# First unit's k and q loaded first and turned ahead of the gates, a and U by VectorE alone, in an mLSTM cell with a multiplicative FFN

## The chip, the cores and the metric

The kernel runs on one core of a Trainium2 chip. TensorE multiplies matrices, VectorE, ScalarE and GpSimd work on tiles in the on-chip memory, SyncE issues transfers. Each engine works through its own list of instructions in order. The metric is the time of one execution on the device, in microseconds; several runs are taken and their median is given.

## What is computed

An mLSTM cell over 4 batches, 8 heads, 768 steps and a head size of 40, whose output, reshaped to 3072 tokens of 320, goes through a multiplicative FFN of width 1024:

```python
for t in range(S):
    m_new = np.maximum(f_gate[:, :, t] + m, i_gate[:, :, t])
    f_stab = np.exp(f_gate[:, :, t] + m - m_new)
    i_stab = np.exp(i_gate[:, :, t] - m_new)
    m = m_new
    C = f_stab[:, :, None, None] * C + i_stab[:, :, None, None] * np.einsum('bhd,bhe->bhde', vt, kt)
    n = f_stab[:, :, None] * n + i_stab[:, :, None] * kt
    h_tilde = np.einsum('bhde,bhe->bhd', C, qt)
    denom = np.maximum(np.abs(np.einsum('bhd,bhd->bh', n, qt)[:, :, None]), 1.0)
    y[:, :, t] = 1.0 / (1.0 + np.exp(-o_gate[:, :, t])) * h_tilde / denom
...
a = x @ w1
b = x @ w2
h = a * b @ w3
return (h @ w_out).astype(np.float32)
```

The inputs of the cell are 32-bit numbers. The four weight matrices are held as 64-bit numbers, and the kernel makes 32-bit ones of them itself.

## The kernel before

**Units and steps.** The cell is worked in chunks. A unit is 128 time steps of one batch with all 8 heads; there are 24 units, and unit n belongs to batch n mod 4. Inside a unit two chunks of 64 steps are done at once in the two halves of the partitions. The main loop (L709) runs over steps s: step s loads unit s + 2, makes the scores and the new state of unit s, the output of unit s - 1, and from step 4 on FFN products for units that are done. Front work before the loop prepares the gates for all units and the weights of unit 0.

**The gates** (L513 to L528). The gates of all heads lie in 96 partitions of 256 columns: a third of the time steps for each of 32 pairs of batch and head. `F` is the running sum of the forget gates in a chunk, `U` a running maximum, `a` the input gates, and `M` the maximum carried from chunk to chunk (`before` is M spread over a chunk). L524 and L525 take M from U and from a, L526 makes the maximum of U and F, L527 takes F from a, and L528 makes U = F - U. L525 and L527 run on GpSimd, the rest on VectorE. What leaves this part is a (`a - before - F`) and U (`F - max(U - before, F)`).

**What is made of them.** `pg` turns a gate tile on TensorE (`gate_cols`, L531), and ScalarE copies it: `aT` from a, later `wT` from w and `gT` from g. `spread` (L265) brings U to all partitions as `ub`, with 32 matmuls for a unit. `weights` (L275) makes `pw`: eight exponentials on ScalarE (L280) from `ub` and `aT`, and two masks on GpSimd (L282). `dec` (L539) gives `pick` on GpSimd (L547) and `pd` on TensorE, from which `decay` is copied (L555). `weighted` (L301) makes `vw` on GpSimd (L304) from v and `wT`.

**Turning k and q.** `turn` (L285) turns k and q of a unit on TensorE (`pt`, four matmuls each, through L95), and ScalarE copies them out as kT and qT (L299).

**The products of a step** (`quarter_work`, L312). For unit s: the scores `cell<-qT,kT`, then the new state's `cell<-vw,kbuf`; the multiplication of the scores by `pw` is VectorE's L355.

**Loads.** SyncE issues the loads. `load(n)` (L125) calls for k, q and v of a unit: each 160 KB, in pieces of 160 bytes (one head of one time step). `fetch` (L203) calls for a weight piece: 512 KB in rows of 4 KB, as 64-bit numbers. `scale` (L178) is ScalarE's part in making 32-bit numbers of a piece, `to_f32` (L180) VectorE's four operations; `scale_next` and `convert` take the pieces in the order in which they were called for. A transfer is issued only after the eighth before it in the list of SyncE's and ScalarE's transfers has landed, since they share eight semaphores in turn; in the front all of these have landed by then.

**Order.** TensorE's instructions keep the order in which they are written (L84). From L511 to step 31 the other engines keep theirs as well (`keep_order`, L499). So the list of ScalarE in the front is, before the change: L178 on the first piece, `dec`, `aT` (two copies), L178 on the second piece, the exponential of w (L544), eight exponentials of `pw`, kT, qT, `wT`, decay, g, L178 on the third piece. TensorE's list: `pg` for aT, `ub`, `pd`, `pt` of k and q, `pg` for wT, the products of unit 0, `pg` for gT, `ub` of units 1 and 2, `pt` of unit 1. SyncE's list: forget gates, weight pieces 1 and 2, k, q, v, o of unit 0, weight pieces 3 to 5, k, q, v, o of unit 1, three stores of U, then the loads of unit 2.

Of the kernel before, what the change touches and what calls it, by code (L numbers as in the profile page):

```python
# [10 lines left out]
AF = mybir.ActivationFunctionType  # L11
OP = mybir.AluOpType
# [4 lines left out]
def kernel(  # L17
# [26 lines left out]
    nc = tc.nc  # L44

    B, H, S, D = q.shape
    L = 64
# [29 lines left out]
    def mps(shape, name):  # L77
        pool = banks.pop(0)
        banks.append(pool)
        return pool.tile(shape, FP, name=name, tag="m")  # L80
# [10 lines left out]
    def mm(out, lhsT, rhs, start=True, stop=True):  # L91
        in_order(nc.tensor.matmul(out, lhsT=lhsT, rhs=rhs, start=start, stop=stop))  # L92

    def transpose(out, in_, n=P):
        in_order(nc.tensor.transpose(out, in_, ident[0:n, 0:n]))  # L95
# [6 lines left out]
    NB, NBQ = 4, 3  # L102
    N_DVE = 10
    q_all = const.tile([P, NBQ * H * DP], FP, name="q_all")
    qbuf = [q_all[:, i * H * DP:(i + 1) * H * DP].rearrange("p (h d) -> p h d", d=DP) for i in range(NBQ)]
    kbuf = [const.tile([P, H, DP], FP, name=f"kbuf{i}") for i in range(NB)]
    vbuf = [const.tile([P, H, D1], FP, name=f"vbuf{i}") for i in range(NB)]
    ident = const.tile([P, P], FP, name="ident")
    state = [[const.tile([P, NP, D1], FP, name=f"state{b}_{i}") for i in range(3)] for b in range(B)]
    aT = const.tile([P, NT2, BH], FP, name="aT")  # L110
# [10 lines left out]
    def rows(src, n):  # L121
        c, b = divmod(n, B)
        return src[b, :, c * P:(c + 1) * P, :].rearrange("h p d -> p h d")

    def load(n):  # L125
        for dst, src in ((kbuf[n % NB][:, :, 0:D], k), (qbuf[n % NBQ][:, :, 0:D], q), (vbuf[n % NB][:, :, 0:D], v)):
            if src is not q or n < N_DVE:
                nc.sync.dma_start(out=dst, in_=rows(src, n))

# [10 lines left out]
    def load_o(n):  # L140
        o_t[n] = io.tile([P, H, D], FP, name="o_in", tag="o_in", bufs=4)
        nc.sync.dma_start(out=o_t[n], in_=rows(o_gate, n))  # L142
# [24 lines left out]
    def raw_tile(n, pieces):  # L167
        raw = idle.pop(0) if idle else wst.tile([128, n, 2], U32, name="raw", tag="raw", bufs=4)
        for r, src in pieces:
            dst = raw[r].rearrange("p n two -> p (n two)")  # L170
            if len(src.shape) == 3:
                dst = dst.rearrange("p (m n) -> p m n", m=2)
            nc.sync.dma_start(out=dst, in_=src)  # L173
        return raw

    def scale(raw):
        hi = raw[:, :, 1].bitcast(FP)
        nc.scalar.activation(out=hi, in_=hi, func=AF.Prelu, scale=2.0 ** -111, alpha=2.0 ** 32)  # L178
# [15 lines left out]
    def cols(c0, n):  # L194
        return slice(2 * c0, 2 * (c0 + n))
# [7 lines left out]
    def fetch(kind, i, part):  # L203

        if kind == "w12":
            c0 = part * CW
            if i < 2 * KF:
                wt, src = ((w1, w1_d), (w2, w2_d))[i // KF]
                ko = i % KF
                dst, pieces = wt[:, ko, c0:c0 + CW], [(every, src[ko * 128:(ko + 1) * 128, cols(c0, CW)])]  # L210
            else:
                dst, pieces = wr[:, c0:c0 + CW], [(slice(j * REM, (j + 1) * REM), src[KF * P:DM, cols(c0, CW)])
                                                  for j, src in enumerate((w1_d, w2_d))]
        elif kind == "wo":
            dst, pieces = wo[:, i, :], [(square, wo_d[j * CQ + i * 32:j * CQ + (i + 1) * 32, :])
                                        for j, square in enumerate(squares)]
        else:
            dst, pieces = None, [(square, w3_d[i * 128 + part * 64:i * 128 + (part + 1) * 64, cols(j * CQ, CQ)]
                                  .rearrange("(m r) n -> r m n", m=2)) for j, square in enumerate(squares)]
        pend.append((dst, raw_tile(dst.shape[-1] if dst is not None else CW, pieces), i, part))  # L220
# [5 lines left out]
    def scale_next():  # L226
        scaled.append(pend.pop(0))
        scale(scaled[-1][1])
# [56 lines left out]
    def turn(n):  # L285


        if n >= N_DVE:
            for src, dst, name in zip(turned_in[n % 2], (kT_t, qT_t), ("kT", "qT")):
                dst[n] = sb.tile([128, NP, P], FP, name=name, tag=name)  # L290
                done = nc.vector.transpose(out=dst[n].rearrange("i p (r f) -> i p f r", f=4),
                                           in_=src[:, 32:TB].rearrange("i (p f d) -> i p f d", p=NP, f=4)[:, :, :, 0:32])
            return done
        for src, dst, name in ((kbuf[n % NB], kT_t, "kT"), (qbuf[n % NBQ], qT_t, "qT")):
            pt = mps([128, NP, P], "pt")
            for p in range(NP):
                transpose(pt[:, p, :], src[:, 2 * p:2 * p + 2, :].rearrange("p a b -> p (a b)"))
            dst[n] = sb.tile([128, NP, P], FP, name=name, tag=name)
            nc.scalar.copy(out=dst[n], in_=pt)  # L299
# [149 lines left out]
    f_sb, a, F, U, on = (gates[0:RG, i * TC:(i + 1) * TC] for i in range(5))  # L449
# [4 lines left out]
    dec = const.tile([RG, GC], FP, name="dec")  # L454
# [7 lines left out]
        nc.scalar.dma_start(out=a[r], in_=i_gate.rearrange("b h s -> (b h) s")[:, cs])  # L462

    w3o_words = w3o.rearrange("p f d -> p (f d)").bitcast(U32).rearrange("p (n two) -> p n two", two=2)
    fetch("w12", 0, 0)
    fetch("w12", 1, 0)
    load(0)
    load_o(0)
    fetch("w12", 2, 0)
    idle += [w3o_words[:, i * CW:(i + 1) * CW] for i in range(2)]  # L470
    fetch("w12", 3, 0)
    fetch("w12", 4, 0)
    load(1)
    load_o(1)

# [33 lines left out]
    f3, F3, U3, a3, w3d = (x.rearrange("p (c t) -> p c t", t=L) for x in (f_sb, F, U, a, w))  # L509
    V = nc.vector  # L510
# [10 lines left out]
        if i + 1 < GR:  # L521
            V.tensor_copy(out=M[third[i + 1], 0:1], in_=M[r, GC:GC + 1])
    before = M[:, 0:GC].unsqueeze(2).to_broadcast([RG, GC, L])
    V.tensor_tensor(out=U3, in0=U3, in1=before, op=OP.subtract)  # L524
    nc.gpsimd.tensor_tensor(out=a3, in0=a3, in1=before, op=OP.subtract)  # L525
    V.tensor_tensor(out=U, in0=U, in1=F, op=OP.max)  # L526
    nc.gpsimd.tensor_tensor(out=a, in0=a, in1=F, op=OP.subtract)  # L527
    V.tensor_tensor(out=U, in0=F, in1=U, op=OP.subtract)  # L528
    for i, r in enumerate(third):
        nc.sync.dma_start(out=U_d[i * GC:(i + 1) * GC].rearrange("c r t -> r c t"), in_=U3[r])  # L530
    def gate_cols(src, dst, copy):  # L531
        pg = mps([P, GC // 2, GR, BH], "pg")
        for c in range(GC // 2):
            transpose(pg[:, c].rearrange("p g r -> p (g r)"), src[:, c * P:(c + 1) * P], RG)
        for c in range(GC // 2):
            copy(out=dst.rearrange("p (g c) r -> p c g r", g=GR)[:, c], in_=pg[:, c])

    scale_next()
    nc.scalar.activation(out=dec, in_=U3[:, :, L - 1], func=AF.Exp)  # L539
    gate_cols(a, aT, nc.scalar.copy)  # L540
    V.tensor_tensor(out=w3d, in0=a3, in1=U3[:, :, L - 1:L].to_broadcast([RG, GC, L]), op=OP.add)
    scale_next()
    convert()
# [2 lines left out]
    for i, r in enumerate(third):  # L546
        nc.gpsimd.tensor_tensor(out=pick[r, :, i, :], in0=pair[r].to_broadcast([BH, B * NP, GC]), op=OP.mult,  # L547
                        in1=dec[r].unsqueeze(1).to_broadcast([BH, B * NP, GC]))
    weights(0)
    pd = mps([P, B * NP * NT], "pd")  # L550
    for x in range(2):
        mm(pd[halves[x]], odd[:, x].to_broadcast([RG, L]), pick.rearrange("p j g c -> p (j g c)"))
    turn(0)
    gate_cols(w, wT, nc.scalar.copy)
    nc.scalar.copy(out=decay.rearrange("p j c -> p (j c)"), in_=pd)  # L555
    nc.scalar.activation(out=g, in_=U, func=AF.Exp)
# [152 lines left out]
    for s in range(len(n_up)):  # L709
        if B <= s + 3 < NU:  # L710
            load_u(s + 3)
        if s + 2 < NU:
            load(s + 2)
            load_o(s + 2)
# [118 lines left out]
```

## Time and profile before

| what | value |
|---|---|
| median of 5 runs | 449.81 us (448.23 to 450.38) |
| the five runs | 449.81, 450.23, 448.29, 448.23, 450.38 us |
| the profiled execution | 448.58 us |
| its span, first to last instruction | 446.9 us |
| TensorE busy | 428.5 us (96% of the span) |
| VectorE, ScalarE, GpSimd busy | 342.5, 134.9, 84.1 us |
| TensorE busy, 0 to 35 us / 35 to 61 us / 61 us to the end | 25.66 / 22.61 / 380.26 us |
| share of the 16 transfer engines busy, same stretches | 0.95 / 1.06 / 0.51 |

The span is divided into stretches in the last two rows: of the 18.4 us in which TensorE is idle, 9.3 lie in the first 35 us, 3.4 in the next 26, and the rest later. The transfer engines are all but full for the first 61 us. A share can pass 1, since packets of one engine overlap.

A line of the timeline has the start of a group of instructions, its duration, the engine, the line of the program, the operation, the tiles written and read, the shapes and a count. In brackets stands how long the engine was idle before, and what ended that. PEld is TensorE's loading of the stationary operand, SPq an issue on SyncE. A wait for several things is put down to the one that came last by the profile, and where that one had long been done, it was another. Where a helper issues all matmuls, they have its line (L92, L95) and are told apart by their tiles.

### The profile page before, as it was taken

What the parts mean: (1) busy time and instruction counts of PE and PEld (TensorE: products, weight loads), DVE (VectorE), ACT (ScalarE), POOL (GpSimd) and SP (SyncE); (2) the same over time, 40 slices, a digit from 0 to 9 for tenths busy, and PEclk for the clock granted to TensorE, in tenths of its full rate; (3) what the DMA queues carried; (4) which work ended last, traced back from release to release, by engine and by line L of the source; (5) the groups of instructions that cost most, each with busy time, mean ns of one, the idle gap of its engine ahead of it and who ended that gap; (6) DMA issues with size and microseconds to landing.
All of it is one profiled execution on the core that took longest, in us unless ns stands there. A gap on an engine that the chain in (4) does not pass through costs nothing.

```text
span 446.9 us, 12911 instructions
## 1 busy us (share of the span) xinstructions
PE 428.5 (96%) x5271; PEld 340.1 (76%) x5271; DVE 342.5 (77%) x703; ACT 134.9 (30%) x376; POOL 84.1 (19%) x156
## 2 busy tenths in 40 slices
PE   2998989998999999999999999999999999999997
PEld 2787778787778878787877878778778777777774
DVE  6698599999998988988876859668698776445800
ACT  3754364443542343143222321203211111001110
POOL 6352233333202220221122203202020000000000
PEclk9999999999999999999999999999999999999999
DMA  8998987989998886686663677374121120000001
GB/s 176 197 167 164 215 155 148 162 183 173 217 192 185 165 174 172 145 173 138 111 114 101 138 151 135 75 131 116 51 37 34 35 50 17 15 16 15 1 29 44
DMA packets 136554, 52.71 MB, mean 118 GB/s; under 512 B 109936, under 2 KB 127536, under 8 KB 136496
## 3 DMA queue, kind: packets, MB, share of 16 engines
q1 hardware_dynamic: 132896, 47.87, 54.7%
q10 hardware_dynamic: 3600, 4.03, 2.6%
q8 instruction: 41, 0.67, 0.7%
q14 instruction: 17, 0.14, 0.1%
HBM read 46.07 MB, written 5.80 MB: 116 GB/s over the span
## 4 chain that ended last, share of the span: by engine, by line
PE 87%; DMA 3%; SPq 3%; DVE 2%; ACT 1%; issue 1%; POOL 1%; DVEq 0%; ACTq 0%; POOLq 0%
PE cell L92 23%; PE pa L92 21%; PE po L92 14%; PE pb L92 14%; PE wp L92 7%; PE p L92 5%; DMA kbuf<-in_k_dram 2%; PE pt L95 2%; PE px L95 1%; DMA raw<-in_moe_w_dram 1%; SPq L173 1%; SPq L142 1%; DVE pw L355 0%; DVE h L382 0%; PE ub L92 0%
## 5 line engine op out<-in xcount | busy, mean ns | idle before, releaser
L92 PE MATMUL pa<-xT,w 128*128 128x256 f32 x240 | 62.3, 391 | 0.7 <-ACT xT L440 0.7
L92 PE MATMUL po<-w3o,ab 128*128 128x320 f32 x224 | 61.8, 433 | 0.0
L92 PEld LDWEIGHTS po<-w3o,ab 128*128 128x128 f32 x224 | 42.4, 190 | 17.3 <-issue 0.4
L309 POOL TENSOR_TENSOR state<-state,decay 128x164 f32<-128x164 f32 x40 | 19.7, 492 | 183.6 <-DVE den L390 170.0
L92 PEld LDWEIGHTS pa<-xT,w 128*128 128x128 f32 x240 | 45.6, 195 | 9.0 <-ACT xT L440 1.6
L92 PE MATMUL pb<-xT,w 128*128 128x256 f32 x192 | 45.7, 381 | 1.5 <-ACT kT L299 1.5
L282 POOL TENSOR_SCALAR_AFFINE_SELECT pw<-pw 64x512 f32<-64x512 f32 x48 | 35.0, 729 | 52.5 <-ACT pw L280 51.0
L92 PE MATMUL cell<-w3o,ab 128*128 128x320 f32 x160 | 44.0, 432 | 0.0
L92 PEld LDWEIGHTS pb<-xT,w 128*128 128x128 f32 x192 | 36.6, 191 | 7.2 <-ACT kT L299 2.3
L280 ACT ACTIVATE pw<-pw,aT 128x64 f32<-128x64 f32 x160 | 40.3, 336 | 2.9 <-ACT o_sb L688 2.4
L633 DVE SCALAR_TENSOR_TENSOR a_sb<-pa,wo 128x512 f32<-128x512 f32 x12 | 8.3, 691 | 42.0 <-PE pa L92 42.0
L92 PEld LDWEIGHTS cell<-w3o,ab 128*128 128x128 f32 x160 | 30.4, 190 | 12.0
L585 ACT ACTIVATE a_sb<-pa 128x512 f32<-128x512 f32 x24 | 14.3, 597 | 77.1 <-PE pb L92 77.1
L92 PE MATMUL pa<-xT,wr 64*64 64x256 f32 x384 | 36.8, 386 | 0.0
L92 PE MATMUL pb<-xT,wr 64*64 64x256 f32 x384 | 36.2, 379 | 0.0
L92 PE MATMUL wp<-wo,w3T 128*128 128x320 f32 x128 | 35.9, 433 | 0.1
L382 DVE TENSOR_TENSOR h<-cell,h 64x164 f32<-64x164 f32 x96 | 31.3, 326 | 1.8
L92 PEld LDWEIGHTS wp<-wo,w3T 128*128 128x128 f32 x128 | 23.7, 190 | 9.2 <-DVE ab L586 0.4
L92 PEld LDWEIGHTS pa<-xT,wr 64*64 64x64 f32 x384 | 19.0, 132 | 14.4 <-issue 8.4
L688 ACT COPY o_sb<-po 128x320 f32<-128x320 f32 x14 | 6.0, 425 | 67.4 <-PE po L92 67.4
L586 DVE TENSOR_TENSOR ab<-pb,a_sb 128x512 f32<-128x512 f32 x24 | 16.1, 686 | 11.3 <-ACT a_sb L585 11.3
L178 ACT ACTIVATE raw<-raw 128x512 f32<-128x512 f32 (+1 forms) x32 | 19.2, 625 | 12.8 <-DMA raw<-in_moe_w_dram 11.0
(124 smaller groups left out, 751.3 us busy)
## 6 DMA issues: line engine op xcount, KB each, us to landing
raw<-in_moe_w_dram SPq DMA_DIRECT2D x64, 128.0 KB, 3.5
pw<-U_d SPq DMA_DIRECT2D x40, 128.0 KB, 4.1
kbuf<-in_k_dram SPq DMA_DIRECT2D x24, 160.0 KB, 4.6
vbuf<-in_v_dram SPq DMA_DIRECT2D x24, 160.0 KB, 4.9
o_in<-in_o_gate_dram SPq DMA_DIRECT2D x24, 160.0 KB, 4.5
out_dram<-o_sb ACTq DMA_DIRECT2D x24, 160.0 KB, 1.8
raw<-in_moe_w_dram SPq DMA_DIRECT2D x7, 512.0 KB, 5.5
raw<-in_moe_w_out_dram SPq DMA_DIRECT2D x32, 80.0 KB, 2.9
```

What stands on the lines that cost most here:

```text
L92: in_order(nc.tensor.matmul(out, lhsT=lhsT, rhs=rhs, start=start, stop=stop))
L95: in_order(nc.tensor.transpose(out, in_, ident[0:n, 0:n]))
L142: nc.sync.dma_start(out=o_t[n], in_=rows(o_gate, n))
L178: nc.scalar.activation(out=hi, in_=hi, func=AF.Prelu, scale=2.0 ** -111, alpha=2.0 ** 32)
L280: nc.scalar.activation(out=pw[:, h, :], in_=src[:, h, :], func=AF.Exp, bias=aT[:, c, b * H + h:b * H + h + 1])
L282: nc.gpsimd.affine_select(out=pw[r], in_=pw[r], compare_op=OP.is_ge, fill=0.0, base=0, pattern=[[0, H], [1, L]], channel_multiplier=-1)
L309: nc.gpsimd.tensor_tensor(out=new, in0=old, op=OP.mult, in1=decay[:, b * NP:(b + 1) * NP, 2 * c + x:2 * c + x + 1] .to_broadcast([P, NP, D1]))
L382: nc.vector.tensor_tensor(out=part, in0=ph[x][halves[e]], in1=part, op=OP.add)
L585: nc.scalar.mul(out=a_sb, in_=pa, mul=UP ** -2)
L586: nc.vector.tensor_tensor(out=ab_t[gr][j][:, fs[0]:fs[-1] + 1, t0:t0 + a_sb.shape[-1]], in0=pb, in1=a_sb, op=OP.mult)
L633: nc.vector.scalar_tensor_tensor(out=out, in0=p, scalar=UP ** -2, in1=q, op0=OP.mult, op1=OP.add)
L688: nc.scalar.copy(out=o_sb, in_=po)
```

## The change

It has three parts, all in the work before the loop.

- SyncE's list begins, after the forget gates, with k and q of unit 0; then come weight piece 1, v, weight piece 2, o and the rest as before.
- `turn(0)` is moved ahead of `gate_cols(a, ...)`: on TensorE `pt` of k and q comes first of all, ahead of `pg` for aT; on ScalarE kT and qT come first. There `dec` now follows aT, and the scaling of weight pieces 1 and 2 follows `dec`, both ahead of the exponential of w.
- a and U are made by four operations on VectorE and none on GpSimd: `before` is added to F, F is taken from a, the lesser of F and U goes into `f_sb`, and U is subtracted from that.

```diff
-    def load(n):
-        for dst, src in ((kbuf[n % NB][:, :, 0:D], k), (qbuf[n % NBQ][:, :, 0:D], q), (vbuf[n % NB][:, :, 0:D], v)):
+    def load(n, which=slice(0, 3)):
+        for dst, src in ((kbuf[n % NB][:, :, 0:D], k), (qbuf[n % NBQ][:, :, 0:D], q), (vbuf[n % NB][:, :, 0:D], v))[which]:
...
+    load(0, slice(0, 2))
     fetch("w12", 0, 0)
+    load(0, slice(2, 3))
     fetch("w12", 1, 0)
-    load(0)
     load_o(0)
...
-    V.tensor_tensor(out=U3, in0=U3, in1=before, op=OP.subtract)
-    nc.gpsimd.tensor_tensor(out=a3, in0=a3, in1=before, op=OP.subtract)
-    V.tensor_tensor(out=U, in0=U, in1=F, op=OP.max)
-    nc.gpsimd.tensor_tensor(out=a, in0=a, in1=F, op=OP.subtract)
-    V.tensor_tensor(out=U, in0=F, in1=U, op=OP.subtract)
+    V.tensor_tensor(out=F3, in0=F3, in1=before, op=OP.add)
+    V.tensor_tensor(out=a, in0=a, in1=F, op=OP.subtract)
+    V.tensor_tensor(out=f_sb, in0=F, in1=U, op=OP.min)
+    V.tensor_tensor(out=U, in0=f_sb, in1=U, op=OP.subtract)
...
+    turn(0)
+    gate_cols(a, aT, nc.scalar.copy)
+    nc.scalar.activation(out=dec, in_=U3[:, :, L - 1], func=AF.Exp)
     scale_next()
-    nc.scalar.activation(out=dec, in_=U3[:, :, L - 1], func=AF.Exp)
-    gate_cols(a, aT, nc.scalar.copy)
     V.tensor_tensor(out=w3d, in0=a3, in1=U3[:, :, L - 1:L].to_broadcast([RG, GC, L]), op=OP.add)
     scale_next()
     convert()
...
-    turn(0)
     gate_cols(w, wT, nc.scalar.copy)
```

## The prediction

> **What bounds the kernel now.** I read the timeline of TensorE first, because TensorE is busy for 428.5 of the 446.9 us span and has work almost without a break from 8.17 us on. Columns here and below: start, duration (both us), engine, line, operation, tiles, count, and in brackets the idle time before it with what ended that.
>
> ```profile
> 8.17 0.58 PE L95 MATMUL pg<-ident,gates 96*128 96x96 f32 x2 [8.17 <-DMA kbuf<-in_k_dram]
> 8.68 1.98 PE L92 MATMUL ub<-gates,ident 96*64 96x64 f32 x32
> ...
> 15.33 1.09 PE L92 MATMUL cell<-vw,kbuf 64*64 64x41 f32 x32
> ...
> 20.72 1.11 PE L95 MATMUL pt<-ident,kbuf 128*128 128x128 f32 x4 [0.17 <-DMA kbuf<-in_k_dram]
> ```
>
> TensorE starts at 8.17 us. The bracket blames a load of k, but `pg` turns the gates and reads no k; the weight load of the same instruction is put down to GpSimd's L527, which ends at 8.12. The second unit's `pt` at 20.72 does wait for a load: its k was called for at 11.87 and took 8.8 us, so it lands at 20.67.
>
> ```profile
> 34.82 1.09 PE L95 MATMUL pt<-ident,kbuf 128*128 128x128 f32 x4 [0.40 <-DMA kbuf<-in_k_dram]
> ...
> 42.07 0.88 PE L92 MATMUL cell<-vw,kbuf 64*64 64x41 f32 x23 [1.53 <-issue]
> ...
> 46.05 3.78 PE L92 MATMUL pa<-xT,w 128*128 128x256 f32 x8 [0.57 <-ACT xT L440]
> ...
> 55.68 1.89 PE L92 MATMUL pa<-xT,w 128*128 128x256 f32 x8
> ```
>
> Two things matter here. At 34.82 TensorE waits 0.40 us for the fourth unit's k: the loads gate the front twice, and a delay of TensorE before that is swallowed up to these waits. And the same eight `pa` products take 3.78 us at 46.05 but 1.89 us at 55.68: until about 49.8 us TensorE works at half its later speed, although the row of granted clock shows 9s throughout.
>
> Next, ScalarE, which is a strict queue in this kernel:
>
> ```profile
> 9.05 0.68 ACT L178 ACTIVATE raw<-raw 128x512 f32<-128x512 f32 x1
> 9.63 0.41 ACT L544 ACTIVATE gates<-gates 96x256 f32<-96x256 f32 x1
> 10.77 1.74 ACT L280 ACTIVATE pw<-ub,aT 128x64 f32<-128x64 f32 x8 [0.73 <-PE ub L92]
> ```
>
> The first unit's exponentials (`pw`, L280) come behind the scaling of the second weight piece (L178). Today that piece is long there and `ub` is what they wait for. GpSimd follows them:
>
> ```profile
> 12.64 1.82 POOL L282 TENSOR_SCALAR_AFFINE_SELECT pw<-pw 64x512 f32<-64x512 f32 x2 [2.04 <-ACT pw L280]
> 14.54 0.73 POOL L304 TENSOR_TENSOR vw<-vbuf,wT 128x328 f32<-128x328 f32 x1
> ```
>
> The masks end at 14.46, `vw` at 15.27, and the products of `vw` start at 15.33. So the path in the front is `ub`, eight exponentials, two masks, `vw`, products.
>
> VectorE's gate chain, with GpSimd's L525 and L527 beside it:
>
> ```profile
> 6.82 0.72 DVE L526 TENSOR_TENSOR gates<-gates 96x256 f32<-96x256 f32 x1
> 7.57 0.83 DVE L528 TENSOR_TENSOR gates<-gates 96x256 f32<-96x256 f32 x1
> 8.50 0.42 DVE L541 TENSOR_TENSOR gates<-gates 96x256 f32<-96x256 f32 x1
> ```
>
> An operation of 96x256 takes 0.42 us alone (L541, L524) and 0.72 to 0.83 beside GpSimd's. Last, the issues (tiles, count, size, us from issue to landing):
>
> ```profile
> vbuf<-in_v_dram SPq DMA_DIRECT2D x1, 160.0 KB, 7.1
> ...
> kbuf<-in_k_dram SPq DMA_DIRECT2D x1, 160.0 KB, 4.7
> ```
>
> The first is the first unit's v, issued at 4.23: landed at 11.3. The second is the third unit's k, issued at 22.53 into an almost empty queue. The same view gives the landings of the others: first weight piece 2.18 + 4.4 = 6.6, second 2.65 + 5.5 = 8.15, k 3.12 + 6.2 = 9.3, q 3.60 + 6.9 = 10.5. They land in the order of issue, a weight piece some 1.5 us after its forerunner and a 160 KB load 0.8 to 1.2 us.
>
> **The change, part by part.**
>
> *a and U by VectorE.* Removed: GpSimd's L525 and L527. VectorE has four operations in place of three. It starts them at 6.36 as now. With nothing of GpSimd beside them each takes 0.42 us plus a gap of 0.04: a is ready at 6.36 + 0.46 + 0.42 = 7.24 (8.12 now), U at 8.16 (8.40 now). Gain: 0.88 us for a, 0.24 for U. Bound: were the 0.72 to 0.83 theirs even without GpSimd, a would come at 7.5 to 7.6 and U at about 9.2.
>
> *k and q called for first.* SyncE issues k at 2.18 and q at 2.65, then the first weight piece, v, the second piece, o. With the rows of the third unit (4.7 and 4.8 us) k lands at 6.9 and q at 7.45; the lower bound is the first piece's own 4.4 less the 0.3 to 0.7 by which a 160 KB step is shorter, some 6.0.
>
> *Turned ahead of the gates.* `pt` is 1.12 + 1.06 us on TensorE: 6.9 to 9.0 (or from 6.0 to 8.1). Then `pg` to 9.5 (8.6) and `ub`, 1.98 us, to 11.5 (10.6); now it ends at 10.66. So the gates' gain is eaten by `pt`, which stands ahead of them, and `ub` ends between the same time and 0.9 us later. The two ScalarE copies of kT and qT (0.59 + 0.58) fall into ScalarE's idle time before 8.4. On ScalarE `dec` now stands behind aT (0.38 us) and the turned copies: at some 10.1 in place of 8.43, so GpSimd's `pick` (1.88 us) ends at about 12.2 and `pd` (0.91) at 13.1, still ahead of the masks and of `vw`. The 2.2 us of `pt` taken out after 11.49 help nothing by themselves: `vw` decides there, as 14.46 for the masks against 14.37 for wT shows.
>
> *The second weight piece.* This is the term that decides. It moves from second to fifth in the queue. The same five transfers that end with v at 11.3 us now will end with this piece, so I take its landing R = 11.3. Bounds: 10.0, if the first two run as short as the shortest step above; 13.6, if both pieces cost the 2.65 us that later ones do (17.8 against 15.2, from 9.87 + 8.0 and 8.67 + 6.5). ScalarE's next entries are L178 on this piece, the exponential of w, then the eight exponentials: now 9.05 to 10.04, so 0.99 us after R. They start at 12.3 in place of 10.77: 1.53 us late. Behind them on ScalarE wait wT, decay and g; for them wait GpSimd's masks and `vw`, and for that TensorE. The masks may be shorter: 1.82 us beside VectorE's conversion, 1.45 at 20.70; I give back 0.2.
>
> *The sum.* The products of `vw` start 1.53 - 0.2 = 1.3 us late. TensorE reached 20.72 with 0.18 us to spare and 34.82 with 0.40; both are used up. That leaves 0.75 us at 34.82, and as TensorE is the path from there (the waits at 42.07 and 46.05 follow from its own work), 0.75 us at the end. The 42.07 wait of 1.53 us has no cause in the profile; were its end fixed in time, it would swallow all of it. VectorE's two conversions, 0.7 us later, still end before their next operation at 16.59, which is itself 1.3 us late. SyncE's later issues are held by the queue and not by compute, so the loads of the next units stay where they are.
>
> *Speed of TensorE.* TensorE is busy for all 5.61 us from 8.17 to 13.78 and 6.34 of 6.41 from 14.13 to 20.54, and stays at half speed; so I count no gain for a denser front. The Trainium skill ("TensorE: Matmul & The Clock Gate", Part 1: The HAM clock gate) says that one busy window of about 3.4 us brings the full rate. This trace disagrees: two longer stretches did not. By the rule, an earlier start at `pt` would raise the speed earlier, and the sum would be a gain where the row gives none.
>
> **Time.** The profiled execution took 448.58 us for a span of 446.9; the five runs have a median of 449.81 and lie between 448.23 and 450.38. All six average 449.25. I start half way between this and the median, at 449.5, and add 0.75: 450.3. A difference of 0.3% (1.35 us) is about what a measurement of this kernel can tell from no change.
>
> **The rivals.**
> - *The loads hide it* (0.13). If R is 10.7 or less, the delay is under 0.7 and the two waits for k swallow it: 449.5. For: those waits. Against: the queue's landing times. It can't gain, because k of units two and four land as before.
> - *The second piece comes later still* (0.34). The mechanism is the same wait on ScalarE, with R at 12.3 as its centre: 2.5 - 0.2 - 0.58 = 1.75 us, so 451.3, or 451.6 from the median. It decides as soon as R passes 11.9, 0.6 us beyond my value. For: later weight pieces take 2.65 us each, and v's issue now hangs 3.58 us in SyncE's queue with the second piece behind it. Against: early pieces took 1.5 us.
> - *TensorE is fast sooner* (0.15). Should the half-speed stretch end before the first `pa` group, that group falls from 3.78 to 1.89 us: 449.5 - 1.9 = 447.6. For: runs 2.15 us apart with nothing else in sight. Against: a front as busy as now did not do it.
>
> **How the numbers follow.** The forecast has 0.38; with the first rival, no change has 0.51. Slower by more than 0.3% 0.34, faster 0.15. The range goes from 448.4, where runs like the quickest shown meet a hidden delay, to 452.0, which takes in the second rival with a run as slow as the slowest.
>
> **What would show it.** Right: `pt` at 6 to 7 us, ScalarE idle before its second L178 until a weight piece lands at about 11.3, L280 at about 12.3, `vw` at about 15.9, `pt` of the second unit at about 22 with no wait for a load, and of the fourth at about 35.6. GpSimd's two operations gone and VectorE's four at 0.42 us. Wrong: L280 before 11; or `pt` of the fourth unit at 34.8; or `pa` products at 0.2 us each before 46.

## The result, and the profile after

The changed kernel takes 447.38 us (median of 31 runs, 445.47 to 449.86). The kernel before has 449.81 us (55 runs, 447.02 to 453.55). The ratio is 0.9949 with a 95% interval of 0.9936 to 0.9962: faster by 0.51%, some 2.3 us. The prediction said 450.3 us, and gave no change a chance of 0.51.

The profiled execution took 446.57 us, with a span of 444.9 us against 446.9.

```profile
PE 422.2 (95%) x5271; PEld 333.3 (75%) x5271; DVE 342.7 (77%) x704; ACT 133.9 (30%) x376; POOL 81.5 (18%) x154
```

The busy times hardly tell what happened. The timeline of TensorE does; its columns are those of the prediction's lines. Units are counted from 0 here: the prediction's second and fourth units are units 1 and 3.

```profile
5.55 1.09 PE L95 MATMUL pt<-ident,kbuf 128*128 128x128 f32 x4 [5.55 <-DMA kbuf<-in_k_dram]
...
8.21 1.98 PE L92 MATMUL ub<-gates,ident 96*64 96x64 f32 x32 [0.21 <-DVE gates L528]
...
15.82 1.09 PE L92 MATMUL cell<-vw,kbuf 64*64 64x41 f32 x32 [2.63 <-POOL vw L304]
...
20.97 1.12 PE L95 MATMUL pt<-ident,kbuf 128*128 128x128 f32 x4
...
33.46 0.66 PE L95 MATMUL pt<-ident,kbuf 128*128 128x128 f32 x4
...
39.05 0.56 PE L92 MATMUL cell<-vw,kbuf 64*64 64x41 f32 x23 [1.07 <-issue]
40.04 0.63 PE L95 MATMUL pt<-ident,kbuf 128*128 128x128 f32 x4 [0.43 <-DMA kbuf<-in_k_dram]
...
42.88 3.78 PE L92 MATMUL pa<-xT,w 128*128 128x256 f32 x8 [0.57 <-ACT xT L440]
```

Read it beside the lines of before. The products of `vw` start at 15.82 us in place of 15.33: the front is later, by 0.49 us. Unit 1's `pt` is still 0.25 us later (20.97 against 20.72). Then the sign turns: unit 3's `pt` starts at 33.46 against 34.82, unit 4's at 40.04 against 42.87, and the first `pa` group at 42.88 against 46.05, which is 3.17 us earlier. So the start of the kernel, which the change edits, got slower, and the gain shows only behind it, clearly from unit 3 on.

ScalarE shows the wait that the prediction was built on:

```profile
8.54 0.66 ACT L178 ACTIVATE raw<-raw 128x512 f32<-128x512 f32 x1
10.52 0.67 ACT L178 ACTIVATE raw<-raw 128x512 f32<-128x512 f32 x1 [1.32 <-DMA raw<-in_moe_w_dram]
11.09 0.41 ACT L545 ACTIVATE gates<-gates 96x256 f32<-96x256 f32 x1
11.39 1.70 ACT L280 ACTIVATE pw<-ub,aT 128x64 f32<-128x64 f32 x8
```

The second L178 stands idle 1.32 us for the second weight piece, and the exponentials (L280) start at 11.39 in place of 10.77: 0.62 us late. On VectorE, the four operations that make a and U take 0.42 us each. Two of them:

```profile
7.28 0.41 DVE L527 TENSOR_TENSOR gates<-gates 96x256 f32<-96x256 f32 x1
7.73 0.42 DVE L528 TENSOR_TENSOR gates<-gates 96x256 f32<-96x256 f32 x1
```

The view that explains the gain is SyncE's, which the prediction did not follow past 12 us. First before, then after; each duration is how long SyncE was held at that issue.

```profile
4.23 3.58 SPq L128 DMA_DIRECT2D vbuf<-in_v_dram  x1
7.85 0.78 SPq L142 DMA_DIRECT2D o_in<-in_o_gate_dram  x1
8.67 1.15 SPq L173 DMA_DIRECT2D raw<-in_moe_w_dram  x1
9.87 1.96 SPq L173 DMA_DIRECT2D w3o<-in_moe_w_dram  x3
11.87 0.86 SPq L128 DMA_DIRECT2D kbuf<-in_k_dram  x1
```

```profile
4.10 0.43 SPq L128 DMA_DIRECT2D vbuf<-in_v_dram  x1
4.58 0.67 SPq L173 DMA_DIRECT2D raw<-in_moe_w_dram  x1
5.30 0.43 SPq L142 DMA_DIRECT2D o_in<-in_o_gate_dram  x1
5.77 2.26 SPq L173 DMA_DIRECT2D raw<-in_moe_w_dram  x1
8.07 1.69 SPq L173 DMA_DIRECT2D w3o<-in_moe_w_dram  x3
9.81 0.63 SPq L128 DMA_DIRECT2D kbuf<-in_k_dram  x1
```

Before, the issue of v holds SyncE for 3.58 us, and unit 1's k is called for at 11.87. After, v's issue takes 0.43 us, the long hold, of 2.26 us, comes at the third weight piece, and unit 1's k is called for at 9.81: 2.06 us sooner. The rest of the list follows it. Unit 2's k is issued at 20.69 (22.53 before), unit 3's at 25.60 (28.72). By the trace's records of the landings, unit 3's k has landed in full at 31.75 us (34.69 before), unit 4's at 39.90 (42.56).

Not all of the 3.17 us reaches the end: from the first `pa` to the end of the span there are 402.0 us after and 400.9 before. About one microsecond of that is TensorE idle between 61 and 100 us (1.66 us after, 0.59 before), and the largest piece of it is a stop of 1.15 us before 87.28, of the kind that is explained below. It is not a constant of the change: the same stretch from the first `pa` to the end was 401.0 us when the changed kernel was profiled again (e14 below), and over the fourteen profiled executions it lies between 399.9 (e2) and 404.1 us (e9). So one profile shows what moved the first `pa`; what that is worth is read from the timed runs.

### The profile page after: what moved, and what is told of

Same layout as the page of the kernel before. It is cut to its first block, busy times and chain, and to the rows that moved or that the text cites. A ratio compares the mean times of both kernels' runs of the same rounds, so it can differ in the third digit from the quotient of the medians.

```text
span 444.9 us, 12907 instructions
## 1 busy us (share of the span) xinstructions
PE 422.2 (95%) x5271; PEld 333.3 (75%) x5271; DVE 342.7 (77%) x704; ACT 133.9 (30%) x376; POOL 81.5 (18%) x154
## 4 chain that ended last, share of the span: by engine, by line
PE 87%; DVE 3%; DMA 3%; POOL 2%; ACT 2%; issue 2%; SPq 1%; DVEq 0%; ACTq 0%; POOLq 0%
PE cell L92 23%; PE pa L92 22%; PE pb L92 14%; PE po L92 14%; PE wp L92 8%; PE p L92 5%; DMA raw<-in_moe_w_dram 1%; DMA q_all<-in_q_dram 1%; PE px L95 1%; PE pt L95 1%; POOL pw L282 1%; ACT pw L280 1%; DVE h L382 1%; DVE pw L355 1%; DVE ab L586 0%
## 5 line engine op out<-in xcount | busy, mean ns | idle before, releaser
L280 ACT ACTIVATE pw<-pw,aT 128x64 f32<-128x64 f32 x160 | 40.2, 337 | 2.9 <-ACT o_sb L688 2.4
L92 PE MATMUL cell<-vw,kbuf 64*64 64x41 f32 x704 | 16.4, 227 | 6.8 <-POOL vw L304 4.0
```

The costliest lines, as they stand in the source:

```text
L280: nc.scalar.activation(out=pw[:, h, :], in_=src[:, h, :], func=AF.Exp, bias=aT[:, c, b * H + h:b * H + h + 1])
```

## The experiments

In the expectations, Theory 1 is that the loads make the gain, Theory 2 that TensorE's speed does, Theory 3 that the wait for the second weight piece still costs time. 1a, 1b and 1c are three forms of Theory 1. Each kernel is set against runs of the kernel before on the same chip, whose median is given with it.

**One part at a time.** e1 is the new order of the loads alone:

```diff
+    load(0, slice(0, 2))
     fetch("w12", 0, 0)
+    load(0, slice(2, 3))
     fetch("w12", 1, 0)
-    load(0)
     load_o(0)
```

> The first part of the change alone: k and q of unit 0 called for ahead of the weight pieces, v between the two pieces; TensorE's and ScalarE's lists and the gates as before. Theory 1 (the loads: v's issue no longer hangs 3.58 us in SyncE's list, so SyncE calls for the later pieces and units some 2 us sooner, and the k of unit 3 lands near 31.8 us in place of 34.7): 2 us or more of the 2.4 us gain comes with this part alone, around 447.5 us against 449.7, even if TensorE stays at half speed until 46 us. Theory 2 (TensorE's speed: the gain comes from TensorE going to full speed near 24 us, which needs the turned list): no gain, 449 to 450 us, with cell products of 32 still at 1.1 us up to 46 us. Theory 3 (the wait for the second weight piece on ScalarE, as in the prediction, costs here as well): scaling of piece 2 starts near 10.5 us, and as ub ends at 10.66 nothing is lost by it.

446.66 us against 448.38, ratio 0.9961 (0.9937 to 0.9984). The whole change's ratio lies in this interval. Unit 1's k lands at 18.17, unit 4's at 40.17, the first `pa` at 43.48.

e2 is `turn(0)` ahead of the gates, with `dec` behind aT, and nothing else:

```diff
+    turn(0)
+    gate_cols(a, aT, nc.scalar.copy)
+    nc.scalar.activation(out=dec, in_=U3[:, :, L - 1], func=AF.Exp)
     scale_next()
-    nc.scalar.activation(out=dec, in_=U3[:, :, L - 1], func=AF.Exp)
-    gate_cols(a, aT, nc.scalar.copy)
...
-    turn(0)
     gate_cols(w, wT, nc.scalar.copy)
```

> The second part alone: turn(0) ahead of the gates on TensorE and ScalarE, dec and the two scalings moved behind, loads called for in the old order, gates shared with GpSimd. k and q land at 9.3 and 10.5 us as before, so pt of q ends near 11.5 and ub near 14. Theory 1: slower by 1 to 3 us (451 to 453 us), since the loads of later units stay where they are and the front is 3 us late. Theory 2: could be faster if the denser list after 9.3 us brings TensorE to full speed before 30 us; then 447 to 448 us.

448.44 us against 448.38, ratio 1.0002 (0.9983 to 1.0020). Theory 1's expectation of 451 to 453 us was a miss, and no gain came either. ScalarE now waits for unit 0's k to be turned, and the exponentials start at 13.87 us:

```profile
10.45 0.58 ACT L299 COPY kT<-pt 128x512 f32<-128x512 f32 x1 [6.95 <-PE pt L95]
...
13.87 1.74 ACT L280 ACTIVATE pw<-ub,aT 128x64 f32<-128x64 f32 x8
```

```profile
18.48 1.09 PE L92 MATMUL cell<-vw,kbuf 64*64 64x41 f32 x32 [2.24 <-POOL vw L304]
...
43.38 1.11 PE L95 MATMUL pt<-ident,kbuf 128*128 128x128 f32 x4
...
46.46 1.99 PE L92 MATMUL pa<-xT,w 128*128 128x256 f32 x8 [0.64 <-ACT xT L440]
```

The products of `vw` start at 18.48, 3.15 us later than before. Yet the first `pa` group starts at 46.46, only 0.41 us later, and the time does not change. The waits that TensorE had in before (0.17 us for unit 1's k, 0.40 for unit 3's, 1.53 at 42.07) are all gone in e2: they took up most of the delay. So a front that is three microseconds late cost nothing here.

e3 is a and U by VectorE alone:

```diff
-    V.tensor_tensor(out=U3, in0=U3, in1=before, op=OP.subtract)
-    nc.gpsimd.tensor_tensor(out=a3, in0=a3, in1=before, op=OP.subtract)
-    V.tensor_tensor(out=U, in0=U, in1=F, op=OP.max)
-    nc.gpsimd.tensor_tensor(out=a, in0=a, in1=F, op=OP.subtract)
-    V.tensor_tensor(out=U, in0=F, in1=U, op=OP.subtract)
+    V.tensor_tensor(out=F3, in0=F3, in1=before, op=OP.add)
+    V.tensor_tensor(out=a, in0=a, in1=F, op=OP.subtract)
+    V.tensor_tensor(out=f_sb, in0=F, in1=U, op=OP.min)
+    V.tensor_tensor(out=U, in0=f_sb, in1=U, op=OP.subtract)
```

> The third part alone: a and U by four operations on VectorE, none on GpSimd. All theories: a is ready near 7.3 us in place of 8.1 and U near 8.1 in place of 8.4, so pg starts at 7.3, ub ends near 10.2 and the first exponentials start 0.3 to 0.5 us sooner. Theory 1: swallowed by the waits for k of units 1 and 3 at 20.7 and 34.8 us, no change (449 to 450 us). Theory 2: no change unless TensorE's speed rises early.

449.68 us against 448.38, ratio 1.0027 (1.0007 to 1.0047): no gain, perhaps a small loss. In its profiled execution the forget gates landed some 1.1 us later than before and VectorE's first scan started at 4.76 us; no reason for that was found, and whether it belongs to the edit stays open.

e6 is the loads with the turn, so the change without the gates.

> The first two parts together, the gates shared with GpSimd as before. The gates' part is worth 0.4 us in ub, which now waits for U and not for pt. Theory 1 and theory 2 both: near the changed kernel, 447.5 us within 0.5; ub starts at 8.4 to 8.7 us, but the exponentials still wait for the second weight piece at 10.5 us, so even these 0.4 us are hidden.

446.59 us, ratio 0.9960 (0.9942 to 0.9978), the same as e1. So the loads' order alone carries the gain, and the two other parts add nothing that can be measured.

**What in the loads' order?** e7 keeps the two weight pieces apart, as the change does, but puts the first one at the head and v behind the second: piece 1, k and q, piece 2, v, o.

```diff
-    fetch("w12", 1, 0)
-    load(0)
+    load(0, slice(0, 2))
+    fetch("w12", 1, 0)
+    load(0, slice(2, 3))
     load_o(0)
```

> The kernel before with only one thing moved: the second weight piece goes between q and v (piece 1, k, q, piece 2, v, o), so no more than two loads of 160-byte pieces stand in a row, as in the change, but the first weight piece keeps the first place and k of unit 0 lands near 8 us. Theory 1a (long rows of 160-byte pieces move slowly, 23 ns a packet after the first thousand or so against 14 to 16; a 4 KB weight piece in between breaks the row): the whole gain of the loads part, o of unit 0 in near 11.1 us, the fifth weight piece near 17 and k of unit 1 near 18.2 (20.67 before), time 446.3 to 447.2 against 448.4 to 449.7. Theory 1b (what counts is that the small loads of k and q stand first): little or no gain, k of unit 1 near 20 us. Theory 2 (TensorE's speed): no gain of itself.

448.74 us against 448.94, ratio 1.0000 (0.9974 to 1.0025): no gain. SyncE is held for 3.13 us at the third piece and calls for unit 1's k at 11.62. Breaking up the row of small loads is not the cause; 1a falls.

e8 puts all four small loads ahead of both pieces.

```diff
+    load(0)
+    load_o(0)
     fetch("w12", 0, 0)
     fetch("w12", 1, 0)
-    load(0)
-    load_o(0)
```

> The kernel before with k, q, v, o of unit 0 called for ahead of both weight pieces: four loads of 160-byte pieces in a row, and all of them first. Theory 1a: no gain in the loads, k of unit 1 at 19.8 us or later and packets of 160 bytes at 20 ns and more from the second thousand on; and as both weight pieces land near 10 to 11.5 us, the exponentials of unit 0 start 0 to 1.5 us late; time like before or up to 0.3% slower. Theory 1b (small loads first): k of unit 1 near 18.2 us and a gain like that of the loads part alone, 0.4%.

447.76 us, ratio 0.9982 (0.9956 to 1.0009): not settled as a time. The loads did come early, against 1a and as 1b has it (unit 1's k is issued at 8.85, unit 4's lands at 39.17), but TensorE then stood still for 2.76 us in the middle of a group, and its first `pa` is at 45.67:

```profile
41.69 0.88 PE L92 MATMUL cell<-vw,kbuf 64*64 64x41 f32 x23 [2.76 <-issue]
```

The 1.53 us before 42.07 in the kernel before is a stop at the same product (the tenth of its group of 32), and after has one of 1.07 us there too. None has a releaser in the timeline, but the trace's records of the transfers show what they wait for: each ends 1.2 to 1.6 us after the end of a transfer of 16 KB which the trace calls "instruction" (it ends at 40.22 us in e8, at 40.45 in before, at 37.81 in after). The same holds for all 26 stops of 0.3 us or more that TensorE makes with no releaser behind the first 14 us of the fourteen profiled executions. They come at few places of its list, above all before the 10th or the 23rd to 24th product of a `cell<-vw,kbuf` group, and where the transfer came sooner, as in e2 and e9, there is no stop at these places. That is TensorE waiting for its own instructions, which come through the same transfer engines as the loads. What decides when that transfer runs was not found.

e11 and e12 part "k and q first" (1b) from "a weight piece late in the list" (1c). e11 has piece 1 first, then k, q and v, then piece 2, o. e12 has k and q first, then both pieces, v, o.

```diff
     fetch("w12", 0, 0)
-    fetch("w12", 1, 0)
     load(0)
+    fetch("w12", 1, 0)
     load_o(0)
```

> The kernel before with one thing moved: the second weight piece goes behind v (piece 1, k, q, v, piece 2, o). The first weight piece keeps the first place. Theory 1c (depth of the queue: SyncE hangs while too many 160-byte pieces are queued; what is still queued when it comes free for the third weight piece decides whether the transfer engines run short at 12 to 14 us; a weight piece late in the list keeps the queue deep): gain in the loads, k of unit 1 at 18.2 to 19.0 us, engines full from 10 to 14 us. Theory 1b (k and q first of all): no gain in the loads, k of unit 1 at 20.2 us or later, as in the run with the pieces apart. In both the second piece lands near 11.3 us and delays the exponentials of unit 0 by 0.5 to 1.5 us; time 448 to 449.5.

> The kernel before with the list k, q, piece 1, piece 2, v, o: k and q first of all, and the last two small loads behind both weight pieces. Theory 1c (depth of the queue): little gain, since v and o are all that is queued when SyncE comes free, as in the kernel before; k of unit 1 near 20 us, engines at 0.8 from 12 to 14 us. Theory 1b (k and q first): k of unit 1 near 18.2 us and a gain of 0.4%, as in the loads part.

e11: 446.89 us against 448.14, ratio 0.9972 (0.9953 to 0.9991). e12: 447.70, ratio 0.9992 (0.9977 to 1.0007). So e12, with k and q at the head, gains nothing that can be told from none and not the 0.4% of 1b, and e11, without them there, gains: 1b falls. (The two intervals overlap; the profiles part the two more clearly, with unit 4's k landed at 42.39 us in e12 and 40.40 in e11.) SyncE in e12:

```profile
4.52 0.43 SPq L128 DMA_DIRECT2D vbuf<-in_v_dram  x1
...
6.07 3.10 SPq L173 DMA_DIRECT2D raw<-in_moe_w_dram  x1
...
10.95 0.72 SPq L128 DMA_DIRECT2D kbuf<-in_k_dram  x1
...
18.92 3.63 SPq L531 DMA_DIRECT2D U_d<-gates  x3
22.59 0.43 SPq L128 DMA_DIRECT2D kbuf<-in_k_dram  x1
```

and in e11:

```profile
3.76 2.23 SPq L128 DMA_DIRECT2D vbuf<-in_v_dram  x1
...
7.32 0.84 SPq L173 DMA_DIRECT2D raw<-in_moe_w_dram  x1
...
9.94 1.03 SPq L128 DMA_DIRECT2D kbuf<-in_k_dram  x1
...
18.98 1.92 SPq L530 DMA_DIRECT2D U_d<-gates  x3
20.94 0.43 SPq L128 DMA_DIRECT2D kbuf<-in_k_dram  x1
```

In both, SyncE is held for some microseconds, though at different issues; that the queue is full then is how the holds are read here, the trace shows only the holds. What differs is what lies in the queue meanwhile. The views by stretch of before and after show the transfer engines then (the last two columns are their mean busy share and the GB/s moved):

```profile
8.00:10.00 2.00, 1.83 (x26) 1.61 (x28) 1.83 (x5) 1.42 (x5) 1.25 (x4) 1.00 1.26 138
10.00:12.00 2.00, 2.00 (x21) 1.27 (x18) 1.84 (x4) 1.27 (x8) 0.60 (x1) 1.00 1.23 223
12.00:14.00 2.00, 1.78 (x9) 1.48 (x7) 1.87 (x3) 1.60 (x6) 1.31 (x2) 1.00 0.80 197
```

```profile
8.00:10.00 2.00, 1.79 (x34) 1.80 (x36) 1.30 (x4) 1.20 (x5) 0.93 (x3) 1.00 1.12 320
10.00:12.00 2.00, 1.28 (x10) 0.49 (x6) 1.84 (x4) 1.48 (x6) 0.00 (x0) 1.00 1.00 308
12.00:14.00 2.00, 1.19 (x33) 0.95 (x32) 1.90 (x4) 2.00 (x11) 0.72 (x2) 1.00 1.00 309
```

Before, the queue at 8 to 12 us holds v and o, 160 KB loads in pieces of 160 bytes: the engines are full but move 138 and 223 GB/s. They land by 11.8; the third weight piece, whose issue is over at 9.82, lands at 15.17, and between 12 and 14 us the engines are busy only 0.80 of the time. After, a 512 KB weight piece lies between and behind them, the engines stay full at 308 to 320 GB/s, the third piece's issue is over at 8.03 and it lands at 12.56. The share between 12 and 14 us is 0.75 in e7 and 0.87 in e12 (no gain), 1.04 in e11 and 1.09 in e8. That fits 1c. Why the engines run at 0.8 with fewer items in the queue was only argued, not shown.

Not all of 1c came true. Unit 1's k landed at 19.41 us in e11, later than the 18.2 to 19.0 that 1c asked for, and at 19.51 in e12, hardly apart; the third weight piece landed at 14.14 in e11 and at 13.60 in e12. The two runs come to the stores of U together (18.98 and 18.92 us) and part there: the stores hold SyncE for 1.92 us in e11 and 3.63 in e12, and unit 2's k is issued 1.65 us apart. So the runs show which orders bring the loads early, and not by what chain. They fit one description: with one small load or none behind the second weight piece (after, e1, e11, e8) the loads come early, with two or more (before, e7, e12) they come late.

**Is it TensorE's speed?** After's TensorE is at full speed from 24 to 41 us (its groups of 32 products take 0.66 us there in place of 1.09), so its speed is a rival to the loads. e9 adds 15 products of the identity with itself to the kernel before, from 1.6 us on, whose results nothing reads.

```diff
+    for _ in range(15):
+        mm(cell[0][:, 0, 0:P], ident, ident)
     f3, F3, U3, a3, w3d = (
```

> The kernel before with 15 products of ident with itself, whose results nothing reads, on TensorE from 1.6 us to about 8 us, when it was idle: they are to bring TensorE to full speed ahead of the front, with the loads as before. Theory 2 and the third rival of the prediction (TensorE's speed makes the gain): faster by 1.9 us or more, 446.5 to 448. Theory 1 (the loads): cell products of 32 take 0.65 us in place of 1.1 in the front, but k of units 1 to 4 still lands at 20.7, 27.2, 34.7 and 42.6, so TensorE only waits more; a gain of 0 to 0.8 us.

449.64 us against 448.94, ratio 1.0012 (0.9989 to 1.0035).

```profile
8.55 1.15 PE L92 MATMUL ub<-gates,ident 96*64 96x64 f32 x32
...
14.47 0.68 PE L92 MATMUL cell<-vw,kbuf 64*64 64x41 f32 x32 [1.21 <-POOL vw L304]
...
20.69 1.11 PE L95 MATMUL pt<-ident,kbuf 128*128 128x128 f32 x4 [1.74 <-DMA kbuf<-in_k_dram]
...
42.46 1.09 PE L95 MATMUL pt<-ident,kbuf 128*128 128x128 f32 x4 [1.60 <-DMA kbuf<-in_k_dram]
...
45.81 3.78 PE L92 MATMUL pa<-xT,w 128*128 128x256 f32 x8 [0.57 <-ACT xT L440]
```

TensorE is fast until 15.6 us (`ub` 1.15 us, not 1.98) and the products of `vw` start 0.86 us sooner. It then waits 1.74 us for unit 1's k and 1.60 us for unit 4's, and the first `pa` comes at 45.81. What TensorE wins, the loads take. This run speeds only the first 15.6 us; for the later stretch there are others. By the clock records e7 and e12 run fast from about 24 to 34 us too (0.63 and 0.68 us for 32 products at 25 us), without a gain, and e13 below has the earliest `pa` of all with TensorE at half speed from 30.3 to 40.5 us (1.04 us for 32 products at 37.37). Theory 2 falls.

**Does the wait for the second piece still cost?** e10 is the whole change with that piece scaled behind unit 0's exponentials.

```diff
     scale_next()
     V.tensor_tensor(out=w3d, in0=a3, in1=U3[:, :, L - 1:L].to_broadcast([RG, GC, L]), op=OP.add)
-    scale_next()
     convert()
...
     weights(0)
+    scale_next()
```

> The changed kernel with the scaling of the second weight piece moved behind the eight exponentials of unit 0 on ScalarE. This tests the step that the prediction took for decisive. If that wait sets the end: the exponentials start near 10.3 us in place of 11.4, the products of vw near 14.8 in place of 15.8, and the time falls by 0.5 to 1 us below the changed kernel, to 446.4 to 446.9 by the runs of the changed kernel so far. Theory 1: the second unit's turning can start no sooner than 18.1 us and later steps wait for k and q of units 3 and 4 (32 and 40.7 us), so the 1 us is swallowed and the time is that of the changed kernel within 0.3 us.

446.28 us against 448.94, ratio 0.9939 (0.9918 to 0.9960). The wait is gone:

```profile
9.70 0.41 ACT L544 ACTIVATE gates<-gates 96x256 f32<-96x256 f32 x1
10.59 1.75 ACT L280 ACTIVATE pw<-ub,aT 128x64 f32<-128x64 f32 x8 [0.48 <-PE ub L92]
```

The products of `vw` start at 14.85, 0.97 us sooner than after's, the first `pa` 0.37 sooner (42.51). The interval overlaps that of the change, so neither a gain of 0.5 us nor none is shown.

e13 is e10 with the three stores of U issued behind the third weight piece, ahead of unit 1's loads, which before they followed; that lets the later loads be issued sooner. e14 is the changed kernel again, on the same chip.

```diff
-    idle += [w3o_words[:, i * CW:(i + 1) * CW] for i in range(2)]
-    fetch("w12", 3, 0)
-    fetch("w12", 4, 0)
-    load(1)
-    load_o(1)
...
         nc.sync.dma_start(out=U_d[i * GC:(i + 1) * GC].rearrange("c r t -> r c t"), in_=U3[r])
+    idle += [w3o_words[:, i * CW:(i + 1) * CW] for i in range(2)]
+    fetch("w12", 3, 0)
+    fetch("w12", 4, 0)
+    load(1)
+    load_o(1)
```

> The changed kernel with the late scaling of the run before, and the three stores of U called for right behind the third weight piece in place of behind the loads of unit 1. In the changed kernel SyncE spends 3.2 us on these stores at 17.5 us while the queue runs empty (0.33 of the engines busy from 20 to 22 us). Theory 1 (the loads set the front): the loads of units 2 to 4 land 1 to 2 us sooner, k of unit 4 at 38 to 39 us in place of 39.9, and the time falls by another 0.5 to 1.5 us, to 444.5 to 446 us. If the loads no longer set the front after the change: the same as the changed kernel with late scaling, 446.3.

> The changed kernel itself once more, to be compared with the run beside it on the same chip: 446.4 to 447.4 us, 0.4 to 0.6% below the kernel before.

e13: 445.59 us against 448.14, ratio 0.9951 (0.9934 to 0.9968). e14: 446.58, ratio 0.9962 (0.9947 to 0.9977). e13's loads are the earliest of all and its first `pa` is at 41.48, but the two intervals overlap: whether it beats the change is not settled.

**All of them in one table.** The columns are read from each profiled execution: when SyncE issues unit 1's k, when unit 4's k has landed, when the first `pa` group starts; the ratio to the kernel before is from the timed runs.

| kernel | k of unit 1 issued | k of unit 4 landed | first `pa` | `pa` less landing | ratio |
|---|---|---|---|---|---|
| before | 11.87 | 42.56 | 46.05 | 3.49 | |
| e3 | 11.95 | 43.53 | 46.82 | 3.29 | 1.0027 |
| e2 | 11.79 | 42.28 | 46.46 | 4.18 | 1.0002 |
| e9 | 11.78 | 42.33 | 45.81 | 3.48 | 1.0012 |
| e7 | 11.62 | 42.98 | 46.42 | 3.44 | 1.0000 |
| e12 | 10.95 | 42.39 | 45.87 | 3.48 | 0.9992 |
| e10 | 10.29 | 39.23 | 42.51 | 3.28 | 0.9939 |
| e11 | 9.94 | 40.40 | 43.74 | 3.34 | 0.9972 |
| after | 9.81 | 39.90 | 42.88 | 2.98 | 0.9949 |
| e1 | 9.78 | 40.17 | 43.48 | 3.31 | 0.9961 |
| e6 | 9.68 | 39.66 | 43.18 | 3.52 | 0.9960 |
| e14 (the change again) | 9.47 | 40.00 | 43.37 | 3.37 | 0.9962 |
| e8 | 8.85 | 39.17 | 45.67 | 6.50 | 0.9982 |
| e13 (stores of U ahead of it) | 11.46 | 38.28 | 41.48 | 3.20 | 0.9951 |

In twelve of the fourteen the first `pa` follows the landing of unit 4's k by 3.0 to 3.5 us, whatever the front did. In eleven of these unit 4's `pt` starts 0.13 to 0.16 us after that landing, so it is the load that lets it go. The twelfth is before:

```profile
42.87 1.11 PE L95 MATMUL pt<-ident,kbuf 128*128 128x128 f32 x4
```

There `pt` follows the landing by 0.31 us and waits for nothing: the stop that ends at 42.07, with the 23 products behind it, ends last by some 0.2 us. Without that stop, as in e9, the load holds `pt` to about the same time. The two others are e2, whose front was three microseconds late, and e8, where the stop of 2.76 us ended last. Every kernel that issues unit 1's k by 10.3 us has unit 4's k by 40.4, and so has e13, which issues the three stores of U ahead of that k and not behind unit 1's loads; the others have it at 42.3 or later. The ratios divide in the same way: 0.9992 to 1.0027 where that k is late, 0.9939 to 0.9982 where it is early.

## Why the prediction was wrong

*The step that failed* is the end of the prediction's sum: "SyncE's later issues are held by the queue and not by compute, so the loads of the next units stay where they are." Its first half fits the runs and its conclusion is wrong: how long SyncE is held depends on what was issued before, and the change reorders exactly that. Unit 1's k moved by 2.06 us in issue and 2.5 us in landing (18.14 against 20.67). The same error stands in the rival "the loads hide it", which was said to be unable to gain "because k of units two and four land as before".

*The path behind 34.82.* The prediction took TensorE's own work for the path from there to the end, and put 0.75 us on it. e2 refutes that by itself: 3.15 us late at `vw`, 0.41 late at `pa`. The prediction put the wait of 1.53 us at 42.07 down to TensorE's own work, with no cause in the profile, and named the alternative (were its end "fixed in time, it would swallow all of it"). The records show a cause, TensorE's instructions: the wait ends 1.6 us after their transfer; and unit 4's k, landed at 42.56, would have held TensorE to nearly the same time. So transfers held the front at three places in before, and not two, and what the change does to the list of loads was the term to work out first.

*The second weight piece.* The mechanism was right, to the instruction: L178 waits, and behind it the exponentials, the masks and `vw`. The size was off. The piece landed at 10.50 us, not 11.3, since the five transfers that end with it came closer together than in the old order; the exponentials were 0.62 us late, not 1.53, and the products of `vw` 0.49, not 1.3. What this wait costs at the end is not settled: e10 takes it away and brings the first `pa` 0.37 us sooner, and no difference in time that is clear of the noise.

*The gates* were right: 0.42 us for each operation without GpSimd beside them, and no gain in the end (e3).

*k, q and the turn.* k landed at 5.41 us, below the predicted 6.0 to 6.9, so `pt` did not hold up the gates: `ub` waited for U alone and started at 8.21, not at the predicted 9.5. The predicted trade, gates against `pt`, did not come about. It didn't matter for the time, as e2 and e9 show for a front later or sooner than this.

*TensorE fast sooner* was a rival that gave a gain, and after does run fast for 17 us before the first `pa`. But the `pa` group itself still takes 3.78 us, so the place that the rival named is not where the gain is, and e9, e7, e12 and e13 take the speed away as a cause. The prediction had no case with the cause that was found: its gains all came through TensorE.

## What to carry to other kernels

When a change reorders the transfers of a list that one engine issues, follow that engine's issues to the end of the stretch that loads gate, not only the transfers that were moved: where the issuer is held, the order of a few transfers moves every load behind them. Before adding up delays at the start of such a stretch, find the last load that its end waits for, and ask whether that load moves; a front 3 us late cost nothing here, and a list 2 us ahead gained 0.4 to 0.5%. Of the orders tried here, those with at most one load of 160-byte pieces behind the second large piece were the good ones; that this holds elsewhere is not shown.

## What the runs showed of the hardware

TensorE's speed comes and goes in the same program. In after's profile it is full from 24.06 to 41.13 us, half to 47.96, and full from then to the last microsecond; in before's it is half until 49.84, although both fronts are about as busy (14.9 and 15.2 of the first 24 us). In e9 the added products brought full speed at 5.33 us, it lasted to 15.57, and the half-speed stretch after it to 49.71. These stretches last 17.07, 6.83, 10.24 and 34.14 us. The Trainium skill ("TensorE: Matmul & The Clock Gate", Part 1: The HAM clock gate) gives a free-running window of 3413 ns; they are 5, 2, 3 and 10 of it, so the grid agrees. The page also says that one busy window of about 3.4 us brings full speed; e9 does not show that between 15.57 and 49.71, where TensorE was busy for 29.6 of 34.1 us, the first 3.43 us of it for 3.39, and stayed at half. Its relation to the time is loose: among after's 31 runs, executions with a mean granted clock of 0.984 or 0.985 took from 445.47 to 448.62 us.
